# First chunk's attention in single precision, gate logits from transposed rows, weights' low halves by TensorE

## The chip, the cores and the metric

One core of a Trainium2 chip runs the whole program. The metric is the time of one execution on the device in microseconds. The core has five engines with a queue each: TensorE (PE, products; PEld is its loading of weights), VectorE (DVE), ScalarE (ACT), GpSimd (POOL) and SyncE (SP, which here issues most DMA transfers).

## The reference

Three stages follow each other; inputs and output are 32-bit floats but for `w_in` and `w_out`, which are stored as 64-bit floats.

```python
# 1: gated linear attention, q, k, v of 4 batches x 8 heads x 768 steps x 40
m_new = np.maximum(f_gate[:, :, t] + m, i_gate[:, :, t])
C = f_stab * C + i_stab * np.einsum('bhd,bhe->bhde', vt, kt)
n = f_stab * n + i_stab * kt
y[:, :, t] = sigmoid(o_gate) * (C @ qt) / np.maximum(np.abs(n @ qt), 1.0)
# 2: x = y as 3072 tokens x 320
h = x @ w_in                       # 320 x 2048
x = (h * sigmoid(h)) @ w_out       # 2048 x 320
# 3: one of 8 experts per token
logits = x @ w_gate
expert_idx = np.argmax(logits, axis=1)
out[mask] = gate_w[mask, None] * (np.maximum(xe @ w1[e], 0.0) @ w2[e])
```

The choice of the expert must be that of the reference, so products keep nearly 32-bit precision. The kernel does this with 16-bit floats in pairs: a value is a high half and a low half (the value less its high half), and a product is three products, high x high, high x low and low x high.

## The kernel before

**Attention.** The 768 steps are 6 chunks of 128. A unit (`unit(t)`, L616) is one chunk of one batch: t = 4 * chunk + batch, 24 units. It loads q, k, v and the output gate as 128 steps x 8 heads x 40. Units 0 to 3 are the first chunk. There `halves` (L648) scales q and k by ACT (L652), casts the high half by ACT (L653) and subtracts by POOL or DVE (L655) into tiles of 8 blocks of 128 columns; `turned` (L600) transposes these by 8 PE transposes (L612) and a copy (L614) in units 0 to 2, by a DMA transpose (L604) from unit 3 on. The scores of 4 heads are 4 products over 120 rows (L724), the decay weights of the first chunk come from products with masks (L680 to L684), DVE multiplies both (L726), ACT and POOL split the result (L730, L732), values are 24 products of 41 columns (L752 to L754) and the state 24 more (L790 to L792, weights of 40 columns). DVE divides and gates (L757 to L780), and the result is transposed for the dense layer.

**Widening of the dense weights.** `conv_in` and `conv_rest` (w_in, 8 + 2 units) and `conv_out` (w_out, 10 units) each load 64-bit values, make 32-bit values by three integer steps on DVE (`narrow`, L836, L839, L842) in a bank of PSUM, cast the high half by ACT (L866 or L75) and subtract it by DVE (L868, L920).

**Fold.** `fold_out` (L925) multiplies w_out with w_gate, so that the second dense product has 8 more columns, which are the logits. For each of 16 pieces of w_out it makes 6 PE transposes (L939, L940), one copy (L942) and 8 products of 8 columns (L949).

**Dense layer.** `l1(t, g)` is 32 products of 128 columns (L990), ACT and DVE apply the gate (L992, L994), ACT and POOL or DVE split (L997, L998); four g per tile t of 128 tokens. `l2(t, g)` is 12 products of 328 columns (L1019 to L1021) that add into one bank over the four g.

**Routing and experts.** After four tiles `route` (L1040) takes the logits, finds the expert by DVE, counts places by two small PE products (L1077, L1078), scales the rows and writes each to its expert's place in `rows_x` by an indirect DMA (L1129). A slot is 128 rows of one expert: a DMA transpose fetches it (L1199), 64 products (L1226) and 24 (L1239 to L1241) compute it, an indirect DMA writes it out (L1256). 28 slots run; five of them (`EARLY`) hold rows known before the last chunk is routed and stand first. The experts' weights are loaded and split while the kernel runs (`load_e`, L1142).

**What sets the order.** Every operation is a call of `op` with its engine, an assumed duration, what it reads and writes, and a rank. `Plan` (L115) lays all of them out in a list per engine by these assumptions, in up to eight passes that change the ranks, and writes the programs in that order. The table `RK` holds the first ranks. Each engine executes its list in order.

Of the kernel before, what the change touches and what calls it, by code (L numbers as in the profile page):

```python
# [20 lines left out]
SQ = 256.0  # L21
# [7 lines left out]
    tiles=19.85, win=71.01, dwin=4.64, wout=-64.58, dwout=5.8, u0=48.58, u1=136.74, u2=-181.17, u3=-847.73,  # L29
    lead1=223.69, lead=261.63, l1c=-202.11, l2c=-47.42, l2=113.07, gates=135.36, load=113.69, state=-161.3, route=-200.66,  # L30
# [83 lines left out]
class Plan:  # L114
# [8 lines left out]
    IDLE, WARM = 1500, 3000  # L123
# [164 lines left out]
def mlstm_moe_kernel(ctx, tc, q, k, v, ig, fg, og, w_in, w_out, w_gate, w1, w2, out):  # L288
# [17 lines left out]
    NO = DM + E  # L306
# [13 lines left out]
    groups = dict(l0=[0, 1], l1=[0, 1, 2], l2=[(3, 0), (4, 128)], s1=[0, 1, 2, 5, 6, 7], at=[5, 6, 7], gt=[2], wt=[2], pg=[(2, 480)])  # L320
# [3 lines left out]
    def bank(kind, *shape):  # L324
# [5 lines left out]
        hi = lo + (128 if kind == "pg" else 1536 if kind in ("wt", "l2") else 2048)  # L330
# [10 lines left out]
    A = [Region(const, f"A{i}", 20992 if i == 3 else 20480) for i in range(8)]  # L341
# [4 lines left out]
    ident16 = const.tile([128, 128], F16, name="ident16")  # L346
    E_t = const.tile([128, NC, BH], F32, name="E_t")
# [15 lines left out]
    X2 = Region(const, "X2", 4 * 1312)  # L363
# [11 lines left out]
    Ks_b = [a4.cut([128, H, 128], F16) for _ in range(2)]  # L375
# [17 lines left out]
    wo_b = [A[3].cut([128, 2, NO], F16) for _ in range(NF)]  # L393
    x2_b = [X2.cut([128, NO], F32) for _ in range(B)]
    row_b = [RO.cut([128, RW], F32) for _ in range(3)]
# [8 lines left out]
    xT_b = [W2.cut([128, 6, 128], F16) for _ in range(5)]  # L404
    hh_b = [[W2.cut([128, 2, 4, 128], F16) for _ in range(2)] for _ in range(2)]
# [16 lines left out]
    wT_b = [A[1].cut([128, 5, 128], F16) for _ in range(2)]  # L422
# [7 lines left out]
    mneg = a6.cut([128, 4, CH], BF16)  # L430

    pe, ve, ac, po, sp = nc.tensor, nc.vector, nc.scalar, nc.gpsimd, nc.sync

# [4 lines left out]
    op("POOL", 1200, c_pool, W=["ident"], rank=-20)  # L438

# [13 lines left out]
    def c_pool3():  # L453
        for x in Qs_b + Ks_b:
            po.memset(x.ap[:, :, 120:128], 0.0)
# [4 lines left out]
    op("POOL", 1500, c_pool3, W=[*Qs_b, *Ks_b, *v_b, *yy_b], rank=-18)  # L460

    def c_pool4():
# [10 lines left out]
        for x in row_b:  # L473
            po.memset(x.ap, 0.0)
        po.memset(row_b[0].ap[:, 385:386], 2.0 * NONE)
    op("POOL", 5000, c_pool4, W=["tok", "ebase", "tri", "cum", "rev", *row_b], rank=90, after=60)

    EARLY = [(0, 0), (0, 1), (1, 0), (1, 1), (1, 2)]

    def fill_rows():  # L480
        sp.dma_start(
            out=rows_x.rearrange("(e r) w -> r e w", e=E)[0:128],
            in_=row_b[0].ap.unsqueeze(1).to_broadcast([128, E, RW]),
        )
    op("SP", 1200, fill_rows, R=[row_b[0]], W=["rows"], rank=120, lag=2500, move=6400, after=120)
    for e, n in EARLY:
        def fill_early(e=e, n=n):
            o = e * ER + 128 * (n + 1)
            sp.dma_start(out=rows_x[o:o + 128, :], in_=row_b[0].ap)
        op("SP", 600, fill_early, R=[row_b[0]], W=["rows"], rank=121, lag=2500, move=800, after=121)  # L490

# [18 lines left out]
    def gates(c0, c1, rk):  # L510
# [49 lines left out]
        ps, kp = bank("gt", 128, 3, n * BH)  # L560
# [39 lines left out]
    def turned(t, a, z, n, rank):  # L600

        flat = a.ap.rearrange("p x c -> p (x c)")
        if t >= B - 1:
            op("SP", 1300, lambda: sp.dma_start_transpose(out=z.ap, in_=flat), R=[a], W=[z], rank=rank,  # L604
               lag=2800, move=225 * n)
# [10 lines left out]
    def unit(t):  # L616
# [6 lines left out]
        qT, kT = qT_b[i2], kT_b[i2]  # L623
        lam = lam_b[i2]
# [6 lines left out]
        for j, (x, d) in enumerate(((k, kr), (q, qr), (v, vr), (og, orr))):  # L631
            def load(x=x, d=d):
                sp.dma_start(out=d.ap[:, :, 0:D], in_=src(x, c, b))
            op("SP", 600, load, W=[d], rank=ld + (0, 0.1, 4, 6)[j], lag=2200, move=1050, after=ld - 10)
        if c > 0:
# [4 lines left out]
            ], R=["lam_d"], W=[*lam], rank=ld + 3, lag=2500, move=1860)  # L640
# [365 lines left out]
    def l2(t, g):  # L1006
        rk = pos(t) + 4 * g + RK["l2c" if t < B else "l2"]
        c, b = divmod(t, B)
        if g == 0:
            yb[t] = bank("l2", 128, NO)  # L1010
# [259 lines left out]
    for t in range(2, B):  # L1270
        unit(t)
# [242 lines left out]
```

## Time and profile before

| | us |
|---|---|
| three runs | 663.04, 663.45, 664.49; median 663.45 |
| profiled execution | 664.25, of which the span from first to last instruction is 662.6 |
| PE busy | 619.2 (93% of the span) |
| DVE busy | 500.8 (76%) |
| ACT busy | 408.4 (62%) |
| POOL busy | 320.8 (48%) |
| DMA moved | 103.27 MB, 156 GB/s on average |

A group's busy time is the time in which at least one of its instructions ran, so neighbours that overlap in a pipeline are not counted twice within a group. A product's own duration is longer than the distance to the next one; costs of runs are taken from distances of starts. The chain that ended last is PE for 81% of the span.

### The profile page before, as it was taken

The numbers are of one execution on the slowest core, as the hardware profiler recorded it, in microseconds if no ns is written. First come the engines' busy times: TensorE is split into PE (matmuls) and PEld (weight loads), VectorE is DVE, ScalarE is ACT, GpSimd is POOL, SyncE is SP. The second block draws the span as 40 slices with busy tenths as digits, with TensorE's granted clock in tenths as the row PEclk, the third lists the DMA queues.
The fourth block names the chain that finished last, engine by engine and source line by source line (L and its number), as shares of the span: only waits on it lengthen the run. The fifth ranks groups of instructions, "written<-read, shape, count | busy, mean of one in ns | idle before, by whom it ended". The sixth has DMA issues, their size and how long they took to land.

```text
span 662.6 us, 21228 instructions
## 1 busy us (share of the span) xinstructions
PE 619.2 (93%) x8493; PEld 526.8 (80%) x8494; DVE 500.8 (76%) x1014; ACT 408.4 (62%) x839; POOL 320.8 (48%) x455
## 2 busy tenths in 40 slices
PE   2488999999999999989999999999999999999992
PEld 2366888878888888878888889888888888888881
DVE  6997698748887899798888978857678675776650
ACT  4776688738797778677878655635335543644430
POOL 3735367727766786576765555421431322223231
PEclk9666799999999999999999999999999999999997
DMA  8999276898987788978955534375398999877710
GB/s 205 236 254 198 57 117 130 179 225 170 174 153 142 131 156 150 148 149 119 177 124 111 102 93 110 103 143 155 105 227 198 225 228 187 207 202 195 173 63 16
DMA packets 255909, 103.27 MB, mean 156 GB/s; under 512 B 193173, under 2 KB 251480, under 8 KB 255800
## 3 DMA queue, kind: packets, MB, share of 16 engines
q1 hardware_dynamic: 236728, 76.55, 60.0%
q10 hardware_dynamic: 16192, 16.59, 8.9%
q0 software_dynamic: 2880, 8.68, 4.1%
q8 instruction: 68, 1.11, 0.7%
q14 instruction: 41, 0.34, 0.2%
HBM read 68.76 MB, written 11.98 MB: 122 GB/s over the span
## 4 chain that ended last, share of the span: by engine, by line
PE 81%; DMA 8%; DVE 5%; ACT 2%; issue 1%; POOL 1%; SPq 1%; ACTq 0%; POOLq 0%; DVEq 0%
PE PS L990 24%; PE PS L1226 13%; PE PS L1019 7%; PE PS L1020 7%; PE PS L1021 7%; PE PS L1239 4%; PE PS L1241 4%; PE PS L1240 4%; DMA SG<-in_moe_w_dram 2%; PE PS L724 2%; DMA X<-in_moe_w_dram 1%; PE PS L939 1%; DMA A<-A 1%; PE PS L940 1%; DMA A<-in_k_dram 1%
## 5 line engine op out<-in xcount | busy, mean ns | idle before, releaser
L990 PE MATMUL PS<-A,A 128*128 128x128 f16 x3072 | 193.2, 221 | 0.6 <-DVE A L994 0.5
L990 PEld LDWEIGHTS <-A 128*128 128x128 f16 x3072 | 179.5, 99 | 4.7 <-issue 0.8
L1226 PE MATMUL PS<-W,A 128*128 128x128 f16 x1792 | 116.5, 219 | 0.4 <-issue 0.2
L1226 PEld LDWEIGHTS <-A 128*128 128x128 f16 x1792 | 108.3, 98 | 8.1 <-issue 0.4
L1019 PE MATMUL PS<-A,A 128*128 128x328 f16 x344 | 104.1, 303 | 0.0
L1021 PE MATMUL PS<-A,A 128*128 128x328 f16 x344 | 104.1, 302 | 0.0
L1020 PE MATMUL PS<-A,A 128*128 128x328 f16 x344 | 104.0, 302 | 0.0
L1256 POOL DMA_INDIRECT out_dram<-W,sid x28 | 29.4, 1052 | 124.2 <-DVE W L1244 52.0
L1228 ACT ACTIVATE W<-PS 128x512 f16<-128x512 f32 x56 | 32.9, 594 | 79.7 <-PE PS L1226 56.5
L992 ACT ACTIVATE A<-PS 128x512 f32<-128x512 f32 x96 | 56.8, 592 | 33.2 <-PE PS L990 24.6
L994 DVE SCALAR_TENSOR_TENSOR A<-A,PS 128x512 f32<-128x512 f32 x96 | 65.0, 679 | 8.3 <-ACT A L992 8.0
L997 ACT CAST A<-A 128x512 f16<-128x512 f32 x86 | 52.5, 613 | 25.1 <-DVE A L994 13.4
L1241 PE MATMUL PS<-A,W 128*128 128x320 f16 x224 | 67.0, 299 | 0.3 <-issue 0.3
L1239 PE MATMUL PS<-A,W 128*128 128x320 f16 x224 | 67.0, 299 | 0.1
L1240 PE MATMUL PS<-A,W 128*128 128x320 f16 x224 | 67.0, 299 | 0.0
L732 POOL TENSOR_TENSOR A<-A 128x512 f16<-128x512 f32 x33 | 39.2, 1190 | 43.4 <-ACT A L730 43.4
L1230 DVE SCALAR_TENSOR_TENSOR W<-PS,W 128x512 f16<-128x512 f32 x56 | 38.2, 688 | 27.9 <-ACT W L1228 27.8
L671 ACT ACTIVATE A<-A,bias_t 128x128 f32<-128x128 f32 x160 | 56.1, 394 | 1.0 <-POOL A L642 1.0
L998 POOL TENSOR_TENSOR A<-A,A 128x512 f16<-128x512 f32 x30 | 35.1, 1168 | 36.4 <-ACT A L997 36.0
L726 DVE SCALAR_TENSOR_TENSOR A<-PS,A 128x512 f32<-128x512 f32 x48 | 32.8, 684 | 21.3 <-PE PS L724 19.9
L998 POOL TENSOR_TENSOR A<-A 128x512 f16<-128x512 f32 x29 | 37.4, 1291 | 23.7 <-ACT A L997 23.7
L1021 PEld LDWEIGHTS <-A 128*128 128x128 f16 x344 | 33.6, 98 | 14.3
(251 smaller groups left out, 1362.5 us busy)
## 6 DMA issues: line engine op xcount, KB each, us to landing
A<-lam_d SPq DMA_DIRECT2D x40, 256.0 KB
SG<-in_moe_w_dram ACTq DMA_DIRECT2D x18, 320.0 KB
A<-in_moe_w_out_dram SPq DMA_DIRECT2D x10, 512.0 KB
SG<-in_moe_w_dram ACTq DMA_DIRECT2D x18, 256.0 KB
SG<-in_moe_w_dram SPq DMA_DIRECT2D x14, 320.0 KB
A<-in_moe_w_in_dram SPq DMA_DIRECT2D x8, 512.0 KB
A<-in_q_dram SPq DMA_DIRECT2D x24, 160.0 KB
A<-in_k_dram SPq DMA_DIRECT2D x24, 160.0 KB
```

What stands on the lines that cost most here:

```text
L671: ac.activation(out=lam[h // 4].ap[:, h % 4, :], in_=x, func=AF.Exp, bias=bias_t[:, c, b * H + h:b * H + h + 1])
L990: pe.matmul(ps[:, f, :], a, x, start=(n == 0), stop=(n == len(terms) - 1))
L992: op("ACT", act(512), lambda: ac.activation(out=th.ap, in_=ps, func=AF.Tanh, scale=0.5 * HS), R=[kk], W=[th], rank=rk)
L994: op("DVE", dve(512), lambda: ve.scalar_tensor_tensor(out=th.ap, in0=th.ap, scalar=1.0, in1=ps, op0=ALU.add, op1=ALU.mult), R=[kk], W=[th] ...
L998: op(DP, dp(512), lambda m: m.tensor_tensor(out=G.ap[:, 1], in0=th.ap, in1=G.ap[:, 0], op=ALU.subtract), R=[th], W=[G], rank=rk + 2, port= ...
L1019: pe.matmul(ps, gh, w[:, 0, :], start=(f == 0), stop=False)
L1020: pe.matmul(ps, gh, w[:, 1, :], start=False, stop=False)
L1021: pe.matmul(ps, gl, w[:, 0, :], start=False, stop=(f == NF - 1))
L1226: pe.matmul(ps[:, jj, :], l, m, start=(n == 0), stop=(n == len(terms) - 1))
L1239: pe.matmul(ps, hh[:, 0, f % 4, :], x[:, 0, :], start=(f == 0), stop=False)
L1240: pe.matmul(ps, hh[:, 0, f % 4, :], x[:, 1, :], start=False, stop=False)
L1241: pe.matmul(ps, hh[:, 1, f % 4, :], x[:, 0, :], start=False, stop=(f == NF2 - 1))
```

## The change

It does the following.

- The first chunk's attention (units 0 to 3) is computed with 32-bit products: q and k are transposed as they are, 4 transposes of 128 x 128 each (pairs of heads in 64 rows each), scores are 8 products over 40 rows (heads of a pair in different rows of the array), values and state 8 products each. The splitting in halves, its tiles and the two transposes by DMA of unit 3 go.
- `fold_out` and its tiles go; `l2` has 320 columns. `route` is now in two parts. The first scales a chunk's rows and splits them, as before, and SP transposes each of the four by DMA; the second forms the logits by 32 products of 8 columns on PE from the transposed rows and goes on as before. The last chunk has rows and tiles of its own.
- For the low halves of w_in and w_out PE subtracts the high half inside PSUM by a product with a negative scaled identity (`rest`), and ACT or DVE casts the result. The parts of `conv_rest` stay. w_in gets a second bank; three products at the start open the banks.
- Seven early slots in place of five (two of expert 2, whose weights are loaded by `load_all` ahead of them); the zero rows of `rows_x` are written by fewer and larger transfers.
- State products of later chunks load 128 weight columns in place of 40.
- The first ranks and some assumed durations have other values, so the lists of all engines are in another order throughout.

```diff
-    lead1=223.69, lead=261.63, l1c=-202.11, l2c=-47.42, l2=113.07, gates=135.36, load=113.69, state=-161.3, route=-200.66,
+    lead1=113.09, lead=1032.66, l1c=-437.46, l2c=-463.45, l2=-163.58, gates=-736.39, load=-73.54, state=-65.11, route=-284.86,
...
-    IDLE, WARM = 1500, 3000
+    IDLE, WARM = 600, 3400
...
-    EARLY = [(0, 0), (0, 1), (1, 0), (1, 1), (1, 2)]
+    EARLY = [(0, 0), (0, 1), (1, 0), (1, 1), (1, 2), (2, 0), (2, 1)]
...
+        def whole_turned(a, z, r):
+            flat = a.ap.rearrange("p h d -> p (h d)")
+            ps, kk = bank("at", 128, 512)
+            def go():
+                for i in range(4):
+                    x = slice(i * 128, (i + 1) * 128)
+                    pe.transpose(ps[:, x], flat[:, x], ident)
...
+        if c == 0:
+            whole_turned(kr, kT, p)
+            whole_turned(qr, qT, p + 0.5)
...
+            def pairs():
+                for j in range(4):
+                    x = slice(j * 128, j * 128 + 128)
+                    for g in range(2):
+                        r = slice(64 * g, 64 * g + D)
+                        pe.matmul(two[g][0][:, j, :], single(kT)[r, x], single(qT)[r, x], start=True, stop=True)
...
+                if c == 0:
+                    pe.matmul(pv[:, h, :], lam[h % 2].ap[:, h // 2, :], vr.ap[:, h, :], start=True, stop=True)
+                    continue
...
+                    if c == 0:
+                        pe.matmul(ps[0:D, h, :], kr.ap[:, h, 0:D], vw.ap[:, h, :], start=True, stop=True)
+                        continue
+                    kh, kl = K.ap[:, h * 128:h * 128 + 128], K.ap[:, h * 128 + D:h * 128 + D + 128]
...
-    cv_b = [PS.cut([128, 512], F32, at=2048 * i) for i in (3,)]
+    cv_b = [PS.cut([128, 512], F32, at=2048 * i) for i in (3, 2)]
...
+    def opened():
+        for x in cv_b + cvo_b:
+            pe.matmul(x.ap, ident16, ident16[:, 0:1].to_broadcast([128, 512]), start=True, stop=True)
...
+    def rest(mid, i, hi, lo, scale, keys, rk):
+        flat = mid.ap if len(hi.shape) == 2 else mid.ap.rearrange("p (a b) -> p a b", a=hi.shape[1])
+        op("PE", 220, lambda: pe.matmul(flat, less[i], hi, start=False, stop=True, skip_group_check=True),
+           R=["less", *keys], W=[mid], rank=rk)
+        op(AD, ad(512), lambda m: scaled(nc, m, lo, flat, scale), R=[mid], W=keys, rank=rk)
...
-        op("DVE", dve(512), lambda: ve.scalar_tensor_tensor(
-            out=w[:, 3:5, :], in0=x, scalar=SWI, in1=w[:, 0:2, :], op0=ALU.mult, op1=ALU.subtract
-        ), R=[mid, k[0]], W=[k[2]], rank=rk)
+        rest(mid, 0, w[:, 0:2, :], w[:, 3:5, :], SWI, [k[0], k[2]], rk)
...
-    def fold_out(q):
...
-            def trans(j=j, ps=ps):
...
-            def fold(j=j, wT=wT):
...
+            op("SP", 1300, lambda b=b, r16=r16: sp.dma_start_transpose(out=xr[b].ap, in_=r16[:, 0:768]),
+               R=[row], W=[xr[b]], rank=rb, lag=2800, move=1270)
+        yield
+        pl, kl = bank("at", 128, nb, E)
+        def logits():
+            h, l = wg16[:, 0], wg16[:, 1]
+            for b in range(nb):
+                z = xr[b].ap
+                terms = [(0, h[:, 0]), (1, h[:, 1]), (2, h[:, 2]), (0, l[:, 0]), (1, l[:, 1]),
+                         (3, h[:, 0]), (4, h[:, 1]), (5, h[:, 2])]
+                for n, (j, w) in enumerate(terms):
+                    pe.matmul(pl[:, b, :], z[:, j, :], w, start=(n == 0), stop=(n == len(terms) - 1))
+        op("PE", 8 * 27 * nb, logits, R=[*xr[0:nb], "wg"], W=[kl], rank=rk + 1.8 * dr)
```

The order on DVE early in the start, when the first units of weights are widened (A_66 are values of w_in, A_67 of w_out, A_71 scores, W_94 gates). Before:

```order
L920 SCALAR_TENSOR_TENSOR A_69<-PS,A_69 128x8x64
L726 SCALAR_TENSOR_TENSOR A_71<-PS,A_71 128x512
L836 TENSOR_SCALAR PS<-A_67 128x512
L842 SCALAR_TENSOR_TENSOR PS<-A_66,PS 128x512
L839 SCALAR_TENSOR_TENSOR PS<-A_67,PS 128x512
L519 SCALAR_TENSOR_TENSOR W_94<-W_94 32x640
L842 SCALAR_TENSOR_TENSOR PS<-A_67,PS 128x512
```

Now (L889, L892, L895 are the three integer steps, L768 the scores):

```order
L892 SCALAR_TENSOR_TENSOR PS<-A_66,PS 128x512
L768 SCALAR_TENSOR_TENSOR A_71<-PS,A_71 128x512 x2
L889 TENSOR_SCALAR PS<-A_67 128x512
L895 SCALAR_TENSOR_TENSOR PS<-A_66,PS 128x512
L892 SCALAR_TENSOR_TENSOR PS<-A_67,PS 128x512
L889 TENSOR_SCALAR PS<-A_66 128x512
L895 SCALAR_TENSOR_TENSOR PS<-A_67,PS 128x512
```

The subtractions of L920 are gone from between the integer steps, and w_in and w_out alternate.

The order on PE at the first unit: before, the start of the list goes on with the fold (A_69 is w_out, A_67 its transposed piece):

```order
L939 MATMUL PS<-ident_75,A_69 128x128
L940 LDWEIGHTS A_69
L940 MATMUL PS<-ident_75,A_69 64x128
L949 LDWEIGHTS A_67
L949 MATMUL PS<-wg_81,A_67 128x8
```

Now the first unit's scores (L758), values (L797) and state (L840) stand with the subtractions for w_out and w_in (L908):

```order
L908 LDWEIGHTS less_77
L908 MATMUL PS<-A_69,less_77 128x512
L758 MATMUL PS<-A_71 128x128 x8
L908 LDWEIGHTS less_76
L908 MATMUL PS<-A_68,less_76 128x512
L797 MATMUL PS<-A_70,A_71 128x41 x8
L840 MATMUL PS<-A_70,A_67 40x41 x8
```

No transposes of weights are left on PE, and each widened unit has one instruction there instead.

The order on SP at the last chunk: before, the fetches of the early slots end and the loads of weights and the tables follow:

```order
L1199 DMA_TRANSPOSE W_94<-rows_x 128x6x128
L1200 DMA xm_126<-rows_x 128x2
L1153 DMA SG<-in_moe_w_dram 128x2x256
L1154 DMA SG<-in_moe_w_dram 64x256
L1155 DMA SG<-in_moe_w_dram 64x256
```

Now the last early fetches are followed by the four transposes of the last chunk's rows (L1110):

```order
L1253 DMA xm_131<-rows_x 128x2
L1252 DMA_TRANSPOSE A_72<-rows_x 128x6x128
L1253 DMA xm_132<-rows_x 128x2
L1110 DMA_TRANSPOSE A_71<-A_72 128x6x128 x4
L1201 DMA X_93<-in_moe_w_dram 128x2x256
```

What moved is that loads behind L1110 wait until the rows are scaled.

## Rows read from the trace of the kernel before

**Rows 1.** The page, 40 slices: busy share in tenths, granted clock, DMA share.

```profile
PE   2488999999999999989999999999999999999992
...
PEclk9666799999999999999999999999999999999997
DMA  8999276898987788978955534375398999877710
```

**Rows 2.** Stretches: length, then busy us per engine, granted clock, DMA share, GB/s.

```profile
0.00:38.06 38.06, 17.01 (x154) 13.28 (x155) 30.51 (x66) 25.55 (x49) 20.80 (x40) 0.79 0.98 238
38.06:99.26 61.20, 55.82 (x729) 44.82 (x729) 49.74 (x93) 45.54 (x91) 27.58 (x47) 0.77 0.74 140
99.26:650.20 550.94, 546.33 (x7614) 468.72 (x7612) 419.96 (x856) 337.29 (x701) 270.06 (x364) 1.00 0.74 155
650.20:662.60 12.40, 0.00 (x0) 0.00 (x0) 0.55 (x1) 0.00 (x0) 2.38 (x4) 0.63 0.06 20
```

**Rows 3.** Groups on PE: busy us, mean ns | idle before, releasers.

```profile
L939 PE MATMUL PS<-ident,A 128*128 128x128 f16 x64 | 11.0, 266 | 4.2 <-ACT A L942 4.0
L940 PE MATMUL PS<-ident,A 128*64 128x128 f16 x32 | 9.1, 284 | 0.0
L612 PE MATMUL PS<-ident,A 128*128 128x128 f16 x66 | 8.5, 301 | 7.6 <-ACT A L777 3.9 <-POOL A L655 2.4 <-ACT A L614 0.9
...
L949 PE MATMUL PS<-wg,A 128*128 128x8 f16 (+1 forms) x128 | 7.0, 170 | 0.8 <-ACT A L942 0.8
```

**Rows 4.** Timeline of PE: start us, busy us; state, values, first dense product.

```profile
22.20 0.22 PE L790 MATMUL PS<-A,A 128*40 128x41 f16 x1 [1.54 <-ACT A L652]
...
23.16 0.22 PE L752 MATMUL PS<-A,A 128*128 128x41 f16 x1
...
38.06 1.55 PE L990 MATMUL PS<-A,A 128*128 128x128 f16 x16
```

**Rows 5.** Timeline of PE: 32-bit products, and 512 columns of 16 bits.

```profile
12.49 0.63 PE L570 MATMUL PS<-A 32*128 32x32 f32 x2
13.05 0.39 PE L612 MATMUL PS<-ident,A 128*128 128x128 f16 x2
...
34.65 1.80 PE L566 MATMUL PS<-ident,W 32*128 32x32 f32 x15
36.38 0.61 PE L680 MATMUL PS<-A,A 128*128 128x512 bf16 x1
36.78 0.31 PE L683 MATMUL PS<-A 128*128 128x128 bf16 x1
```

**Rows 6.** Groups on DVE, and its timeline at the eighth product group.

```profile
L920 DVE SCALAR_TENSOR_TENSOR A<-PS,A 128x512 f16<-128x512 f32 x10 | 6.8, 684 | 2.2 <-ACT A L75 2.2
L868 DVE SCALAR_TENSOR_TENSOR A<-PS,A 128x512 f16<-128x512 f32 x8 | 5.4, 681 | 3.2 <-ACT A L866 3.2
...
L942 DVE COPY A<-PS 128x640 f16<-128x640 f16 x3 | 1.5, 492 | 3.1 <-PE PS L940 2.0 <-PE PS L949 1.1
...
99.26 0.68 DVE L994 SCALAR_TENSOR_TENSOR A<-A,PS 128x512 f32<-128x512 f32 x1
```

**Rows 7.** Groups on PE with 328 and with 320 columns.

```profile
L1019 PE MATMUL PS<-A,A 128*128 128x328 f16 x344 | 104.1, 303 | 0.0
...
L1239 PE MATMUL PS<-A,W 128*128 128x320 f16 x224 | 67.0, 299 | 0.1
```

**Rows 8.** Timeline of PE: products of 8 columns, a run of 24.

```profile
81.45 0.42 PE L949 MATMUL PS<-wg,A 128*128 128x8 f16 x8
...
261.98 0.20 PE L790 MATMUL PS<-A,A 128*40 128x41 f16 x1
...
262.58 0.18 PE L792 MATMUL PS<-A,A 128*40 128x41 f16 x1
```

**Rows 9.** SP: transposes by DMA; landing times of transfers with rows_x.

```profile
L604 SPq DMA_TRANSPOSE A<-A x63: 1212/1247/4469, 56.3 to 418.5; - x63
...
DMA to landing us min/median/max: 2.9/4.2/6.8
```

More of the change, by code (lines that the diff above doesn't have):

```diff
@@ L339, in pos @@
         return T0 + TT * t
-    A = [Region(const, f"A{i}", 20992 if i == 3 else 20480) for i in range(8)]
+    A = [Region(const, f"A{i}", 20640 if i == 4 else 20480) for i in range(8)]
     home = [0, 1, 4, 5, 6, 2, 3, 7]
@@ L346, in mlstm_moe_kernel @@
     ident16 = const.tile([128, 128], F16, name="ident16")
+    less = [const.tile([128, 128], F16, name=f"less{i}") for i in range(2)]
     E_t = const.tile([128, NC, BH], F32, name="E_t")
@@ L438, in mlstm_moe_kernel, with c_less @@
     op("POOL", 1200, c_pool, W=["ident"], rank=-20)
+    def c_less():
+        for x, y in zip(less, (SWI, SWO)):
+            ac.activation(out=x, in_=ident16, func=AF.Copy, scale=-1.0 / y)
+    op("ACT", 600, c_less, R=["ident"], W=["less"], rank=-10)
     def c_pool2():
@@ new lines, in whole_turned @@
+        def whole_turned(a, z, r):
[5 more added lines that the diff above has]
+                    pe.transpose(ps[:, x], flat[:, x], ident)
+            op("PE", 4 * 110, go, R=[a, "ident"], W=[kk], rank=r)
+            op(AD, ad(512), lambda m: (m.copy if m is ac else m.tensor_copy)(out=single(z), in_=ps),
+               R=[kk], W=[z], rank=r)
@@ L1009, in l2 @@
         if g == 0:
[L1010 removed]
+            yb[t] = bank("l2", 128, DM)
         ps, kk = yb[t]
@@ new lines, in route, with count, place @@
+        op("DVE", 760, hot, R=["rev"], W=[(kr, "ld"), ("oh", c, b0)], rank=rk + 2.2 * dr)
+        def count():
+            for t in range(t0, t1):
+                ve.tensor_tensor(out=cum[:, t + 1, :], in0=cum[:, t, :], in1=oh[:, t, :], op=ALU.add)
+        op("DVE", 170 * nb, count, R=[("oh", c, b0)], W=["cum"], rank=rk + 2.4 * dr)
+        pr, kk = bank("at", 128, nb, E)
+        def place():
+            pe.matmul(pr, ones, cum[:, T, :], start=True, stop=False)
+            pe.matmul(pr, tri, oh[:, T, :], start=False, stop=True)
@@ L1135, in send @@
                 puts.append(p_)
-            op("POOL", 1050, send, R=[row, (kr, "di"), "rows", "early"], W=[("put", t)], rank=rb, lag=2500, move=600)
+            op("POOL", 1050, send, R=[row, (kr, "di"), *filled, "early"], W=[("put", t)], rank=rb, lag=2500, move=600)
     stcount = [0]
@@ L1313, in mlstm_moe_kernel @@
                 load_e(e, g, we_b[e], x, 12)
+        if t == B or t == NTT - 1:
+            for x in row_b[2:] if t == B else row2_b:
+                op("POOL", 80, lambda x=x: po.memset(x.ap.bitcast(F16)[:, 704:768], 0.0), W=[x], rank=pos(t) - 8)
         if t % B == 0 and t > 0:
-            route(t // B - 1, 0, B, pos(t) + RK["route"], 1.0)
-            if t == NTT - B:
+            ways = route(t // B - 1, 0, B, pos(t) + RK["route"], 1.0)
+            next(ways)
+        if t % B == 1 and t > 1:
+            next(ways, None)
+            if t == NTT - B + 1:
                 pc, kc = bank("at", 128, E)
@@ L1338, in mlstm_moe_kernel @@
         l2(NTT - 1, g)
-    route(NC - 1, 0, B, pos(NTT) + 12, 0.5)
+    for _ in route(NC - 1, 0, B, pos(NTT) + 12, 0.5):
+        pass
     end0 = pos(NTT) + 10
     for n, (e, i) in enumerate(early):
+        if e > 1 and e != early[n - 1][0]:
+            load_all(e, end0 + 2 + TS * n)
         slot(i, we_b[e], end0 + 2 + TS * n)
```

332 lines of the change are left out of this document (163 added, 169 removed).

## The prediction

> **What bounds the kernel now.** I read the 40 slices first, then the four stretches, then PE's groups, then the two instruction lists of PE and DVE in the first 100 us. The slices [rows 1] show PE at 9 tenths from the fifth slice to the last but one, with a granted clock of 0.6 to 0.7 in slices 2 to 5, a mixture of the two levels 1.2 and 2.4 GHz, and 2.4 GHz after that. The stretches [rows 2] put numbers on it. PE is busy 546.33 of the 550.94 us between 99.26 and 650.20, so what shortens this part must take work off PE or start it earlier. The last 12.40 us hold no PE work and the change does not touch them. PE's idle time lies in front: 21.05 us up to 38.06, where the first product of the dense layer starts [rows 4], and 5.4 us from there to 99.26. In this second stretch PE is busy 55.82 us at a granted clock of 0.77, and DVE is busy 49.74 of 61.20 us: DVE widens weights there, and PE fills the time with work that is there only because of the gate's fold [rows 3].
>
> I take as a milestone the eighth product group of the dense layer to reach DVE. It starts at 99.26 [rows 6]. After it PE has no gap to speak of, so the end moves by what this milestone moves, plus what the later PE work gains or loses.
>
> **The change, part by part.**
>
> *Fold removed.* The 96 transposes and 128 small products of the fold are busy 11.0, 9.1 and 7.0 us, 27.1 in all, and PE waited 5.0 us in front of them, mostly for the copies of their results [rows 3]. All of it lies before 99.26. With it go 16 copies, 13 on ACT and 3 on DVE of 0.49 us [rows 6].
>
> *First chunk, half precision removed.* Of the 66 transposes of L612 48 are of q and k, 48/66 of 8.5 is 6.2 us [rows 3]. State and value products come as runs of 24: one run is 23.16 - 22.20 = 0.96 us [rows 4], eight runs 7.7. Scores: 32 products at some 0.1, 3.2. Together 17.1 us. ACT and POOL lose the splitting in halves, which only shortens the chain to the first product.
>
> *First chunk, single precision added.* 32 transposes, 32 score products, 64 value and state products, 128 instructions. The trace has few such rows [rows 5]: 15 transposes of 32 x 32 from 34.65 to 36.38, 0.115 us each; one 32 x 32 product, recorded as two instructions, from 12.49 to 13.05, 0.56 us with its hand-over at both ends, 0.28 per record. For a transpose of 128 columns I take 0.23 (between 0.115 and four times that), 7.4 us. For a score product I take 0.28, since two of 40 rows each stand in different rows of the array, 9.0 us (0.14 to 0.56). For a value or state product of 41 columns I take 0.28 as well, since they stand in runs of eight and the hand-over is paid once, 17.9 us (0.115 to 0.56). The sum is 34.3 us; by the low ends 15.6, by the high ends 68.4.
>
> The row for one 32 x 32 product shows two records and two weight loads. The Trainium skill says (TensorE: Matmul & The Clock Gate, "LDWEIGHTS (loading the stationary operand)" and "Weight-path perf modes — Fast Weight Load (FWL) and DoubleRow") that a load of 128 columns takes about 107 ns and that the fast load is not used for 32-bit weights. That sets a floor under this part at either clock: an estimate from the page is 2 x 107 = 214 ns for a product even when nothing else holds it, 13.7 us for the 64. By the row it is 17.9, by the page the forecast would be some 4 us lower and could fall no further.
>
> *Low halves by PE.* The subtraction of the weights' high halves leaves DVE: 18 instructions, 10 of L920 and 8 of L868, 0.684 us each, 17 of them before 99.26, which is 11.6 us; DVE had waited 2.2 + 3.2 us in front of them for ACT [rows 6]. In their place stand 18 PE products of 512 columns, 36.78 - 36.38 = 0.40 us each at the low clock [rows 5], 7.2 us, and 18 evictions that ACT or DVE takes; in DVE's new order 3 of them stand ahead of the eighth product group, 2.0 us. ACT takes the others, about 0.6 us each, out of what it got back. The three products that open the banks run before anything else is ready and cost nothing; if they were late, 1.2 us.
>
> *What that does to the milestone.* DVE ahead of the eighth group: 11.6 + 1.5 - 2.0 = 11.1 us less work, and 5.4 us less waiting if ACT is no longer late, 16.5 in all. PE: 27.1 + 17.1 - 34.3 - 7.2 = 2.7 us less work and 5.0 less waiting, 7.7. The milestone follows the slower of the two in any one place, and PE partly has idle time to hide in. I take 12 us, the middle of 7.7 and 16.5. This is the one large term and is an estimate.
>
> *The dense layer's second product.* 320 columns in place of 328: by the rows of both shapes [rows 7] 104.1/344 goes to 67.0/224, 302.6 to 299.1 ns, and 3.5 ns x 1152 = 4.0 us less, all of it in the stretch that PE fills.
>
> *Logits from transposed rows.* 192 products of 8 columns on PE. Eight of the fold's at 81.45 are busy 0.42 us [rows 8]; 24 such runs are 10.1 us. In a run of 32 the ends are paid once: a run of 24 at full clock takes 0.026 per product (first to last start 262.58 - 261.98 = 0.60 us) [rows 8], so the ends are 0.42 - 8 x 0.026 = 0.21 and a run of 32 is 1.04, six runs 6.2 us. I take 6.2; between 5.0 (no ends) and 10.1.
>
> *24 more transposes by DMA.* SP issues four per chunk at 1.247 us, 5.0 us in which the loads behind them wait [rows 9]; the loads of a unit are issued well ahead, so this costs nothing where they stay so, and up to 5 us once where they don't. POOL's work is the same but for its order. The wait that is added is PE's, for the four transposed tiles. A row that SP writes or reads lands 2.9 to 6.8 us after its issue [rows 9]. From the last product of a chunk to its logits go two steps of ACT, three of DVE, one of POOL, four issues and a landing: some 3.5 + 5 + 4 to 7 us, 13 to 16. Between the two PE has its other products in the new order, 16 us of them in the last chunk and 18 to 30 in the others by the durations of before. So it is hidden, with nothing to spare at the end; I take 1.5 us. In the last chunk seven slots in place of five stand ready before the others need it.
>
> The rest (pads, zero rows, the split of the gate's weights, tables of fetches, 128 weight columns in place of 40 for state, whose records are spaced alike) I cost at nothing: each is hidden beside PE at 546.33 of 550.94. The new loads' order puts the first layer's weights ahead of the second's; it is within the 12 us.
>
> The sum, against the profiled execution's own 664.25 us: 664.25 - 12 - 4.0 + 6.2 + 1.5 = 655.95. The median of the three runs is 0.8 lower, and so is the forecast: **655 us**.
>
> **The rivals.**
>
> *The clock comes early.* PE ran its 55.82 us of the second stretch at 0.77 [rows 2]. With the fold and its waits gone PE has fewer gaps and its products come densely. If it reaches full clock in that stretch, 55.82 x 0.23 = 12.8 us are to be had, some 8 of them beyond my 12: 647. For it speaks that the granted clock is 0.77 for the stretch and 1.00 for all that follows, where PE has no gaps [rows 2]; against it that the single-precision work of four units is spread over the same time.
>
> *Single precision is dear.* If score, value and state products cost 0.56 us, 96 of them are 26.9 us more, PE becomes the bound of the start, and some 10 of the 26 us of idle time absorb a part: 7.7 - 16.9 makes the milestone 9 us later, 664.25 + 9 + 3.7 - 0.8 = 676. From about 0.42 us each the kernel is slower than before. For it speaks the only row there is; against it that this row is a lone product.
>
> *The logits wait.* If PE stands for 2 us or more in each chunk, because SP's queue or a busy DMA brings the tiles late, 6 x 2 are lost on top: 667. For it speaks the DMA share of 7 to 9 tenths up to half of the span [rows 1], against it the PE work that the order puts between.
>
> *The loads set the start.* The DMA share is 0.98 up to 38.06 [rows 2] and the bytes stay the same. If weights come no earlier, the milestone moves 3 us and the rest eats it: 664. Against it: the share falls to 0.74 in the second stretch, where most of the widening is done.
>
> **How the numbers follow.** My case gets 0.55, the early clock 0.20, dear single precision 0.10, waiting logits 0.08, loads 0.07. My case's own range is 649 to 661. The range of 8 in 10 reaches from 644 (early clock with the low prices) to 667 (waiting logits, loads). A difference under 0.2%, 1.3 us, is about what a measurement here cannot tell from none. Faster: my case, the early clock and half of the loads' case, 0.78; within 0.2% 0.05; slower 0.17.
>
> **What would show it.** The eighth eviction of the dense layer's products should start at about 87 us, PE should be free of the fold, and no wait of PE for the transposed rows should pass 2 us. The single-precision products should stand in runs of eight that take about 2.2 us. The milestone at 96 or later, or runs of eight over 3.4 us, would make the forecast wrong; so would a gap of PE over 5 us anywhere after 100 us.

## The result, and the profile after

The changed kernel takes 668.94 us (median of 20 runs, 664.00 to 675.59), the kernel before 664.31 (20 runs, 662.16 to 667.06). The ratio is 1.0062, with a 95% interval of 1.0044 to 1.0080: it is slower by 0.6%, where 655 us were forecast. One of the 20 runs (675.59) and one of the four of e5_xm (677.55) were in a slower state and count in no ratio. The profiled execution took 669.95 us; its span is 668.3 us, 5.7 more than the span before.

The slices of the changed kernel's page, as [rows 1]:

```profile
PE   3888999999899999999999999959799999999993
...
PEclk9996999999999999999999999969899999999997
DMA  8996687999999898997799544372734899878820
```

The start is better than before: PE is at 8 tenths from the second slice. Two holes have come, in the 27th and the 29th slice, where [rows 1] have nines, and the clock falls there.

The clock's digits of the first slices do not tell PE's speed. The first record of the granted clock in this trace is at 41.51 us (18.61 in the trace of before), and where there is none the views count full clock. The products themselves show the low level up to 41.5: one unit's 32-bit scores (16 records) take 2.35 us ahead of it and 1.16 us behind it.

```profile
19.02 2.35 PE L758 MATMUL PS<-A 40*128 40x128 f32 x16
...
41.70 1.16 PE L758 MATMUL PS<-A 40*128 40x128 f32 x16
```

The stretches of the changed kernel (length, then busy us on PE, PEld, DVE, ACT, POOL, granted clock, DMA share, GB/s): up to the first dense product, up to the eighth product group at DVE, up to 425 us, the stretch with the holes, the experts, the tail.

```profile
0.00:32.90 32.90, 19.93 (x101) 13.42 (x102) 27.21 (x57) 13.44 (x27) 9.56 (x33) 1.00 0.96 227
32.90:88.58 55.68, 51.19 (x558) 43.80 (x558) 45.09 (x87) 38.80 (x80) 17.76 (x38) 0.88 0.76 168
88.58:425.00 336.42, 329.32 (x5026) 287.91 (x5024) 280.49 (x595) 246.97 (x553) 214.94 (x274) 1.00 0.85 161
425.00:480.00 55.00, 42.22 (x489) 34.93 (x488) 22.78 (x40) 17.31 (x31) 10.85 (x16) 0.89 0.57 117
480.00:657.10 177.10, 176.86 (x2267) 152.52 (x2264) 115.52 (x225) 73.32 (x116) 44.88 (x79) 0.99 0.69 170
657.10:668.30 11.20, 0.00 (x0) 0.00 (x0) 0.35 (x1) 0.00 (x0) 1.89 (x4) 0.60 0.06 20
```

The first product of the dense layer starts at 32.90 (38.06 before [rows 4]), the eighth group at 88.58 (99.26 before [rows 6]): the milestone moved by 10.7 us, 12 were forecast. Behind it nothing of this is left. Between 425 and 480 PE is busy 42.22 of 55 us, where [rows 2] had 546.33 of 550.94 for everything behind the milestone.

The time can be split without a remainder. PE's own time, counted by the distance from one start to the next without the waits, is 619.7 us before and 620.0 now; it contains what PE loses at the low clock level. PE's waits of over 0.15 us are 26.1 and 17.5 us up to the milestone, 3.8 and 6.7 from there to some 425 us, 0.6 and 12.7 behind that, and the tail behind PE's last product is 12.4 and 11.4. So the span grew by 0.3 - 8.6 + 2.9 + 12.1 - 1.0 = 5.7 us. The question is the 12.1.

The longest waits of PE (total, times, longest), and below them the three holes on its timeline (start, busy; in brackets the wait before it):

```profile
PE PS L1018 <- DVE A L1022: 6.1, 3, 5.1
PE PS L1292 <- DVE W L1297: 4.9, 1, 4.9
PE PS L1047 <- ACT A L1025: 2.7, 1, 2.7
```

```profile
435.64 1.06 PE L1018 MATMUL PS<-A,A 128*128 128x128 f16 x16
441.77 1.87 PE L1018 MATMUL PS<-A,A 128*128 128x128 f16 x16 [5.08 <-DVE A L1022]
446.39 0.45 PE L1047 MATMUL PS<-A,A 128*128 128x320 f16 x1 [2.75 <-ACT A L1025]
...
478.52 0.42 PE L1292 MATMUL PS<-A,W 128*128 128x320 f16 x1 [4.87 <-DVE W L1297]
```

The run of 16 products behind the first hole takes 1.87 us in place of 1.06: PE is at the lower clock level there until some 451 us. Counted by distances, the products behind the holes cost some 4.4 us more than the same products elsewhere, so the holes cost 12.7 + 4.4 = 17.1 us.

DVE and ACT are named as releasers, but neither was busy. ACT's timeline at the first two holes shows who kept them (ACTq are transfers that ACT issues):

```profile
429.06 0.60 ACT L1020 ACTIVATE A<-PS 128x512 f32<-128x512 f32 x1 [0.48 <-PE PS L1018]
433.09 0.38 ACTq L1201 DMA_DIRECT2D SG<-in_moe_w_dram  x1
438.53 0.48 ACTq L1202 DMA_DIRECT2D SG<-in_moe_w_dram  x1
439.11 0.55 ACTq L1203 DMA_DIRECT2D SG<-in_moe_w_dram  x1
439.76 0.54 ACTq L1204 DMA_DIRECT2D SG<-in_moe_w_dram  x1
440.40 0.60 ACT L1020 ACTIVATE A<-PS 128x512 f32<-128x512 f32 x1 [10.74 <-issue]
440.90 0.61 ACT L1025 CAST A<-A 128x512 f16<-128x512 f32 x1
441.75 0.37 ACTq L1201 DMA_DIRECT2D SG<-in_moe_w_dram  x1
443.92 0.47 ACTq L1202 DMA_DIRECT2D SG<-in_moe_w_dram  x1
...
445.72 0.62 ACT L1025 CAST A<-A 128x512 f16<-128x512 f32 x1 [4.21 <-DMA SG<-in_moe_w_dram]
```

ACT issues two groups of four loads of expert weights (`load_e`). The four instructions themselves take 2 us, but ACT stands in front of the first and the second for 3.4 and 5.1 us, and the eviction L1020 behind them, for which PE waits, comes at 440.40. What the loads wait for is in the program's list of waits. The kernel's framework has eight semaphores for all transfers of SP and ACT and uses them in turn; a transfer waits until the one eight places ahead of it, which used the same semaphore, has landed. At this place ACT's list reads (a wait named DMAHW is one of the eight):

```
L1020 ACTIVATE A_73<-PS 128x512 [waits PE_49,Activation_49]
L1201 DMA SG<-in_moe_w_dram 128x2x256 [waits DMAHW4_49,DVE_49]
L1202 DMA SG<-in_moe_w_dram 64x256 [waits DMAHW7_49]
L1203 DMA SG<-in_moe_w_dram 64x256 [waits DMAHW0_49,DVE_49]
L1204 DMA SG<-in_moe_w_dram 128x2x320 [waits DMAHW2_49,DVE_49]
L1020 ACTIVATE A_72<-PS 128x512 [waits PE_49,Pool_49]
```

The transfers eight places ahead are those of SP's early fetches of rows (L1252 a transpose, L1253 a small copy), which start only when the rows have been put, at 429.85. The chain that ended last runs through them:

```profile
426.08 3.75 DMA rows_x<-W,di
429.85 1.23 SPq L1252
431.12 0.56 SPq L1253
431.74 1.21 SPq L1252
...
433.62 1.21 SPq L1252
...
439.97 3.92 DMA A<-rows_x
443.92 0.47 ACTq L1202
...
467.59 7.22 DMA A<-A
474.83 0.47 ACTq L1202
```

The load at 433.09 waits for the copy issued at 431.12, the one at 438.53 for the third transpose (433.62), the one at 443.92 for the sixth (439.97 + 3.92 = 443.89). The trace records the semaphores, too, and bears this out: the copy lands at 433.01 and the third transpose at 438.51, each on the semaphore that the load behind it uses next. The third hole is the same again with the four transposes that the new routing gave to SP (L1110): the last is issued at 467.59 and lands at 474.81, ACT's second load follows at 474.83, and ACT's eviction behind them, for which DVE and PE wait, at 476.69.

In the kernel before, ACT's loads stand beside SP's fetches as well:

```profile
440.92 0.61 ACT L997 CAST A<-A 128x512 f16<-128x512 f32 x1
442.15 0.42 ACTq L1153 DMA_DIRECT2D SG<-in_moe_w_dram  x1
...
445.51 0.37 ACTq L1156 DMA_DIRECT2D SG<-in_moe_w_dram  x1
445.92 0.62 ACT L997 CAST A<-A 128x512 f16<-128x512 f32 x1 [4.39 <-DMA SG<-in_moe_w_dram]
```

There ACT stood for 4.39 us and PE had no wait: its list held enough other products.

### The profile page after: what moved, and what is told of

Its sections match the earlier page's. It is cut to its first block, busy times and chain, and to the rows that moved or that the text cites. A ratio compares the mean times of both kernels' runs of the same rounds, so it can differ in the third digit from the quotient of the medians.

```text
span 668.3 us, 21038 instructions
## 1 busy us (share of the span) xinstructions
PE 619.5 (93%) x8435; PEld 532.6 (80%) x8435; DVE 491.4 (74%) x1001; ACT 389.8 (58%) x804; POOL 299.9 (45%) x441
## 4 chain that ended last, share of the span: by engine, by line
PE 70%; DVE 10%; DMA 9%; SPq 3%; issue 3%; ACT 3%; POOL 2%; ACTq 1%; POOLq 0%; DVEq 0%
PE PS L1018 18%; PE PS L1279 14%; PE PS L1049 6%; PE PS L1047 6%; PE PS L1048 6%; PE PS L1292 4%; PE PS L1294 4%; PE PS L1293 4%; DMA A<-A 4%; DMA A<-in_k_dram 2%; DVE A L768 1%; PE PS L766 1%; SPq L1252 1%; DVE A L1022 1%; PE PS L758 1%
## 5 line engine op out<-in xcount | busy, mean ns | idle before, releaser
L1018 PE MATMUL PS<-A,A 128*128 128x128 f16 x3072 | 196.4, 222 | 6.5 <-DVE A L1022 6.1
L1279 PE MATMUL PS<-W,A 128*128 128x128 f16 x1664 | 107.1, 220 | 0.0
L1047 PE MATMUL PS<-A,A 128*128 128x320 f16 x344 | 103.5, 301 | 2.7 <-ACT A L1025 2.7
L1049 PE MATMUL PS<-A,A 128*128 128x320 f16 x344 | 103.5, 301 | 0.1
L1048 PE MATMUL PS<-A,A 128*128 128x320 f16 x344 | 103.5, 301 | 0.0
L1020 ACT ACTIVATE A<-PS 128x512 f32<-128x512 f32 x96 | 56.5, 592 | 44.2 <-PE PS L1018 21.5
L1022 DVE SCALAR_TENSOR_TENSOR A<-A,PS 128x512 f32<-128x512 f32 x96 | 64.6, 678 | 20.7 <-ACT A L1020 20.1
L1026 POOL TENSOR_TENSOR A<-A 128x512 f16<-128x512 f32 x32 | 38.9, 1216 | 48.0 <-ACT A L1025 47.7
L768 DVE SCALAR_TENSOR_TENSOR A<-PS,A 128x512 f32<-128x512 f32 x48 | 32.5, 684 | 18.7 <-PE PS L766 13.5
L1026 POOL TENSOR_TENSOR A<-A,A 128x512 f16<-128x512 f32 x26 | 33.4, 1286 | 24.2 <-ACT A L1025 24.1
L777 POOL TENSOR_TENSOR A<-A 128x512 f16<-128x512 f32 x27 | 33.1, 1228 | 24.7 <-ACT A L775 24.5
```

The lines of the kernel that those rows point to most:

```text
L1018: pe.matmul(ps[:, f, :], a, x, start=(n == 0), stop=(n == len(terms) - 1))
L1020: op("ACT", act(512), lambda: ac.activation(out=th.ap, in_=ps, func=AF.Tanh, scale=0.5 * HS), R=[kk], W=[th], rank=rk)
L1022: op("DVE", dve(512), lambda: ve.scalar_tensor_tensor(out=th.ap, in0=th.ap, scalar=1.0, in1=ps, op0=ALU.add, op1=ALU.mult), R=[kk], W=[th] ...
L1026: op(DP, dp(512), lambda m: m.tensor_tensor(out=G.ap[:, 1], in0=th.ap, in1=G.ap[:, 0], op=ALU.subtract), R=[th], W=[G], rank=rk + 2, port= ...
L1047: pe.matmul(ps, gh, w[:, 0, :], start=(f == 0), stop=False)
L1048: pe.matmul(ps, gh, w[:, 1, :], start=False, stop=False)
```

## The experiments

Theory A is what was just read: the turns of the semaphores hold ACT, and the evictions behind it hold PE. Theory B: the transfers are slow there whoever issues them. Theory C: the refitted order as such costs the time. Theory D: ACT can issue nothing while SP's transposes are under way. Each number below is a median, with the ratio to the kernel before on the same chip.

### e1_sp: three groups of loads issued by SP

```diff
-        self.out = sorted(best[1], key=lambda x: x[0])
+        moved = {2378, 2383, 2480}
+        self.out = [(t, end, i, "SP" if i in moved else e) for t, end, i, e in sorted(best[1], key=lambda x: x[0])]
```

> Three of the groups of four loads of expert weights that ACT issues beside SP's fetches of rows and transposes (at 433.1, 441.8 and 474.3 us of the changed kernel) are issued by SP at the same place of the order; nothing else moves. Theory A (ACT stands in its queue until the transfer of SP eight places earlier has landed, because SP and ACT use the same eight semaphores in turn, and the evictions behind it hold PE): PE's 12.7 us of idle time between 436 and 479 us go, and with them some 4.4 us in which PE ran at the low clock after each gap: 668.9 - 17 = 652 us, between 649 and 656; ACT stands less than 2 us at a time between 425 and 480. Theory B (the transfers themselves are slow there, since transposes and loads share the DMA engines, and it does not matter who issues them): the weights land as late as before, PE waits for them or for the rows: 665 to 672.

Measured: 649.28 us (5 runs, 648.59 to 651.75), ratio 0.9794 (0.9771 to 0.9817). Theory A's number, and faster than both kernels. The same stretches of its profile, from its own eighth group on:

```profile
87.27:425.00 337.73, 331.41 (x5066) 290.23 (x5064) 283.80 (x599) 250.11 (x558) 216.60 (x276) 1.00 0.87 162
425.00:480.00 55.00, 55.00 (x758) 48.36 (x756) 32.46 (x73) 21.54 (x39) 16.02 (x26) 1.00 0.64 145
480.00:636.40 156.40, 156.16 (x1960) 133.47 (x1958) 103.75 (x190) 66.95 (x105) 38.08 (x66) 1.00 0.76 179
```

PE is busy 55.00 of 55 us where it was 42.22, at the full clock. Only twelve loads differ, in their issuer and, by it, in their time and turn: SP issues the first four from 423.95 us on, ahead of its first fetch, and the next four from 431.16 on, between its second fetch and its third. Theory B is out: those four land 2.9 to 4.1 us after their issue, the first four of ACT in the changed kernel 2.4 to 3.3, so the transfers are not faster here, but no eviction stands behind them.

PE's list is the same product by product, so the two profiled executions can be laid side by side. The one of e1 is 2.9 us ahead at 420 us, where the lists have not differed yet, and 20.9 ahead at 485: the holes cost 18.0 us, 17.1 of which were read above.

### e2_late: ACT keeps the loads, behind the dense layer's last evictions

```diff
+        for ops, mark in (((2378, 2383), 2258), (tuple(range(2379, 2383)) + tuple(range(2384, 2388)), 2299)):
+            mine = [x for x in out if x[2] in ops]
+            out = [x for x in out if x[2] not in ops]
+            n = 1 + next(n for n, x in enumerate(out) if x[2] == mark)
+            out[n:n] = mine
```

> ACT keeps its loads, but the two groups at 433.1 and 441.8 us stand behind the last evictions of the dense layer in ACT's order, and the casts of these weights behind the first evictions of the experts; the third group (474.3 us) stays. Theory A: the first two gaps of PE (5.1 and 2.75 us, and some 2.8 us of low clock behind them) go, the third (4.9 us and 1.6) stays or moves: 668.9 - 10.6 = 658, between 655 and 663. Theory B: the loads are later still, PE waits for weights: 668 or more.

Measured: 656.99 us (6 runs, 653.97 to 658.44), ratio 0.9895 (0.9871 to 0.9918). Two holes are gone, one of 4.8 us is left (PE waits for the evictions of a slot at 456 us). As theory A had it: the loads are later and the kernel is faster, because what PE waits for stands ahead of them.

### e3_early5: five early slots

```diff
-    EARLY = [(0, 0), (0, 1), (1, 0), (1, 1), (1, 2), (2, 0), (2, 1)]
+    EARLY = [(0, 0), (0, 1), (1, 0), (1, 1), (1, 2)]
```

> One part undone: five early slots as in the kernel before, in place of seven; all lists are laid out anew for it. Theory A: SP has ten transfers in place of fourteen at that place and expert 2's weights are not wanted there, so ACT's loads wait less: PE idle between 425 and 480 us under 6 us in place of 12.7, 658 to 665. Theory B: the same gaps, 667 to 671. Theory C (the new first ranks are worse for the whole program): nothing gained, 667 to 672.

Measured: 668.23 us (6 runs, 667.41 to 673.08), ratio 1.0078 (1.0051 to 1.0105). A miss for theory A's time: PE's waits between 425 and 480 fell to 5.5 us as expected (busy 49.55 of 55), but waits of 3.4 and 1.3 us came at 169 and 187 us and 2.7 and 1.2 us at 482 and 500, in the newly laid out lists. The hold itself is still there, only elsewhere on ACT:

```profile
423.62 0.37 ACTq L1201 DMA_DIRECT2D SG<-in_moe_w_dram  x1
424.02 0.54 ACTq L1202 DMA_DIRECT2D SG<-in_moe_w_dram  x1
432.99 0.47 ACTq L1203 DMA_DIRECT2D SG<-in_moe_w_dram  x1
```

By the list of waits the third load is in turn behind the small copy that belongs to SP's first fetch. SP issues that copy at 430.85, since it waits for the rows itself; ACT stands from 424.6 on, six us before that transfer has even been issued. So the number of fetches is not the lever, and a turn passes on whatever the transfer ahead in it waits for.

### e4_ranks: the first ranks of the kernel before

```diff
-    tiles=19.85, win=310.54, dwin=120.43, wout=56.12, dwout=-21.22, u0=-372.07, u1=-36.9, u2=-978.22, u3=-878.97,
+    tiles=19.85, win=71.01, dwin=4.64, wout=-64.58, dwout=5.8, u0=48.58, u1=136.74, u2=-181.17, u3=-847.73,
...
-    IDLE, WARM = 600, 3400
+    IDLE, WARM = 1500, 3000
```

> One part undone: the table of first ranks and the two assumed durations of the kernel before, with all else of the change. Theory C (the refit of the order costs the time): 655 or less. Theory A: the ranks are not the cause as such; the new lists put other work beside SP's fetches, so the time follows the gap that PE has there, between 658 and 675, and PE's idle time between the first put of chunk 4 and the first early slot accounts for the difference to e1.

Measured: 675.83 us (6 runs, 672.96 to 682.27), ratio 1.0194 (1.0156 to 1.0233). Theory C is out. Theory A's range was left by 0.8 us, and its account was too narrow: the eighth group starts only at 110.11, PE waiting 15.9 us for the casts of ACT ahead of the new subtractions, so most of the loss is at the start. ACT is held here too, from 447.1 to 457.0. The refit of the order is worth some 20 us at the start to the new code.

### e5_xm: the small copies on POOL

```diff
     def fetch_slot(row0, rk, keys, i=None):
+        m = sp if i is None else po
...
-            sp.dma_start(out=xm, in_=r[:, 384:386])
+            m.dma_start(out=xm, in_=r[:, 384:386])
```

> The changed kernel, ACT's loads where they were; only the seven small transfers (128 x 2) that follow SP's early row fetches are issued by POOL, which has semaphores of its own. So ACT's loads of the first two groups take their turn behind other transfers: the second to fourth load of the first group behind the first, second and third row fetch, those of the second group behind the fourth to seventh. Theory A (turns of eight semaphores): the first group ends some 3 us earlier, the second not later than the landing of the seventh fetch; PE's first gap 1 to 3 us in place of 5.1, the second near 0, the third as before: 660 to 664; each load of ACT starts when the named fetch has landed. Theory D (no issue of ACT goes through while SP's transposes are under way): all eight loads of ACT start after the last of the seven fetches has landed, and the gaps stay: 667 to 670.

Measured: 673.93 us (4 runs, 667.09 to 677.55), ratio 1.0131 (1.0095 to 1.0168). The time is a miss: the first hole went, but the second grew to 6.1 us, and the third is 4.3 in the profiled execution, which took 667.09 us; why the other runs are slower by up to 10 us no profile shows. The starts of ACT's loads decide between A and D all the same:

```profile
432.10 0.48 ACTq L1202 DMA_DIRECT2D SG<-in_moe_w_dram  x1
...
433.82 0.41 ACTq L1204 DMA_DIRECT2D SG<-in_moe_w_dram  x1
...
437.38 0.39 ACTq L1201 DMA_DIRECT2D SG<-in_moe_w_dram  x1
...
441.81 0.38 ACTq L1204 DMA_DIRECT2D SG<-in_moe_w_dram  x1
```

The landing of the seventh fetch, in the chain that ended last:

```profile
437.12 4.58 DMA A<-rows_x
```

SP issues the seven transposes from 428.08 to 437.12, the last landing 4.58 us later at 441.70 (437.12 + 4.58). The first group of ACT's loads goes out in the middle of them, and the very last load follows the seventh landing by 0.1 us, its place in the turns. By the trace's semaphores each of the seven loads that the expectation pairs with a fetch starts 0.02 to 0.1 us after that fetch has landed, the three of the first group after 432.08, 432.93 and 433.74. Theory D is out. The turns also explain the second hole: ACT's second group now waits for the last four fetches.

### e6_before: control, the kernel before with its group issued by SP

```diff
+        moved = {2451}
+        self.out = [(t, end, i, "SP" if i in moved else e) for t, end, i, e in sorted(best[1], key=lambda x: x[0])]
```

> Control: in the kernel before, the one group of loads that ACT issues beside SP's fetches (442.2 us) is issued by SP, as in the first experiment. Theory A: ACT's wait of 4.4 us there goes, but PE had work in front of it and no gap, so nothing is gained: 663 to 666, within 0.2% of before. If it gains over 1%, the wait cost the kernel before as well and the change did not expose it.

Measured: 665.76 us (12 runs), 666.24 for the kernel before beside it, ratio 0.9984 (0.9971 to 0.9997). As expected within 0.2%: the hold costs only where PE has nothing in front of it. With the hold taken out of both, the change is worth 0.9794 / 0.9984 = 0.981, some 12.6 us.

### e7_dve: the low halves by DVE again

```diff
-        op("PE", 220, lambda: pe.matmul(flat, less[i], hi, start=False, stop=True, skip_group_check=True),
+        op("PE", 220, lambda: None,
...
-        op(AD, ad(512), lambda m: scaled(nc, m, lo, flat, scale), R=[mid], W=keys, rank=rk)
+        op(AD, ad(512), lambda m: ve.scalar_tensor_tensor(
+            out=lo, in0=mid.ap if len(hi.shape) == 2 else flat, scalar=scale, in1=hi, op0=ALU.mult, op1=ALU.subtract
+        ), R=[mid], W=keys, rank=rk)
```

(On top of e1's edit; all of these instructions are put on DVE.)

> The first experiment's kernel, but the low halves of w_in and w_out are again subtracted by DVE straight out of PSUM (one instruction in place of PE's product and an eviction), in the same place of the lists. By the prediction DVE sets the start: ahead of the eighth product group DVE gets some 14 instructions of 0.68 us more, 9 us, and PE loses 6.4 us of work: the eighth group 5 to 10 us later than in the first experiment, 653 to 659. Rival (PE sets the start): the eighth group at the same time or up to 6 us earlier, 644 to 650.

Measured: 654.46 us (5 runs), ratio 0.9823 (0.9797 to 0.9849), against 0.9794 for e1. The eighth group starts at 87.98, against 87.27 in e1. Ahead of it DVE is busy 7.9 us more, and PE has 13 products less. The 0.7 us at the milestone speak against DVE alone as the bound (5 to 10 were expected), but the time lies in the range of DVE's case and not in the rival's, and the milestone differs by some 4 us between executions of one list (last section). So neither engine is shown to set the start alone. In time the part is worth 0.3%, with intervals that overlap.

### e8_double: the first chunk's value and state products issued twice

```diff
-                    pe.matmul(pv[:, h, :], lam[h % 2].ap[:, h // 2, :], vr.ap[:, h, :], start=True, stop=True)
+                    for _ in range(2):
+                        pe.matmul(pv[:, h, :], lam[h % 2].ap[:, h // 2, :], vr.ap[:, h, :], start=True, stop=True)
...
-                        pe.matmul(ps[0:D, h, :], kr.ap[:, h, 0:D], vw.ap[:, h, :], start=True, stop=True)
+                        for _ in range(2):
+                            pe.matmul(ps[0:D, h, :], kr.ap[:, h, 0:D], vw.ap[:, h, :], start=True, stop=True)
```

(On top of e1's edit.)

> The first experiment's kernel, with each of the first chunk's single-precision value and state products issued twice: 128 more records, 12.6 us of PE by the changed kernel's rows. If PE bounds the start, the eighth group is 10 to 13 us later and the time 659 to 662; if these products stand in PE's idle time of the start (17 us up to the eighth group), 3 to 7 us later, 652 to 657.

Measured: 662.02 us (12 runs, 660.52 to 665.93), ratio 0.9952 (0.9932 to 0.9971), which is 0.0158 or 10.5 us over e1. The eighth group starts at 94.51, 7.2 us later. The added products take 11.5 us by distances. In time most of them count, so PE's work in the start is not hidden; the 7.2 at the milestone are in doubt by the same 4 us and lie just above the second expectation.

## Why the prediction was wrong, point by point

**The step that failed** is the one that moves work to SP: "The loads of a unit are issued well ahead, so this costs nothing where they stay so, and up to 5 us once where they don't", with 1.5 us for all stalls. It named the queue of SP and the loads behind L1110 in it. It did not ask who else takes turns with SP's transfers. ACT does, and behind ACT's loads stand the evictions that PE waits for. The runs show 12.7 us of waits and 4.4 us at the lower clock in its place; taking twelve loads off ACT gives back 17.8 us by the ratios to the kernel before (1.0062 and 0.9794; 19.7 between the medians), for the 17.1 read from one trace. The rest of the change was worth more than forecast: 12.6 us by e1 and e6, where 8.3 were added up. The forecast's condition, "a gap of PE over 5 us anywhere after 100 us" would make it wrong, is what came (5.08).

None of the rivals had this. The one that waits for the logits gave 667, near the measured time, by another mechanism: PE's longest wait for the transposed tiles is 0.73 us (L1122 in the rows of groups below), well under the 2 us that it needed. Its transposes did cost time, but through ACT's turn (the third hole).

**The milestone** was right in size, 10.7 for 12, and half wrong in its reason. "The milestone follows the slower of the two" took 16.5 us on DVE's side into the middle. In e7 7.9 us more of DVE's work, with PE relieved, moved it by 0.7; in e8 11.5 us more of PE's moved it by 7.2 and the time by 10.5. So PE's work counts, and DVE's is not shown to. PE's own time up to the milestone fell by 2.1 us (forecast 2.7), its waits by 8.6. That the 2.1 is near the 2.7 is in part luck: with the same list up to there e1 and e2_late have 66.6 and 67.8 us of own time, this execution 71.1 (73.2 before), since PE ran at the low level for different stretches.

**The terms on PE**, by distances of starts over the whole span, forecast and measured (at whatever clock level they ran): fold -27.1 and -22.0; half precision of the first chunk -17.1 and -16.1; single precision +34.3 and +24.9; subtractions +7.2 and +6.6, with 1.5 for the opening products that were forecast at nothing; 320 columns -4.0 and -4.3; logits +6.2 and +5.0. The busy time of groups, from which the fold's 27.1 came, counts the end of each run and is too high by a fifth for short runs. The rows of single precision in the changed kernel:

```profile
L797 PE MATMUL PS<-A,A 128*128 128x41 f32 x64 | 9.5, 314 | 0.0
...
L758 PE MATMUL PS<-A 40*128 40x128 f32 x64 | 5.8, 323 | 0.0
L1122 PE MATMUL PS<-wg,W 128*128 128x8 f16 x160 | 4.9, 166 | 0.7 <-DMA W<-W 0.7
L840 PE MATMUL PS<-A,A 128*40 128x41 f32 x64 | 3.7, 221 | 0.0
```

Each product stands as two records. By distances of starts the 32 value products (L797, 128 weight columns) take 9.06 us, 0.283 each. That this is the forecast's 0.28 is luck, since it is a mean over both clock levels: the first unit's eight, at the low level, take 3.73 us, 0.467 each, those of the other units 1.70 to 1.86 us, 0.21 to 0.23 each. A score product (L758) takes 5.63 / 32 = 0.176 in the mean, a state product (L840), with 40 weight columns, 3.54 / 32 = 0.111.

The run of 3.73 us is over the 3.4 us that the prediction named as a sign against it, but single precision did not make the kernel slower: all of it cost 24.9 us where 34.3 were forecast. The rival of dear single precision is out: the 96 products take 0.19 us in the mean, and only the eight at the low level pass its 0.42. The forecast took its rates of single precision from [rows 5], where the 15 transposes stand at a granted clock of 0.50, and did not reckon with the level.

The Trainium skill's floor (TensorE: Matmul & The Clock Gate, "LDWEIGHTS (loading the stationary operand)") goes by the weights' columns; the prediction applied its 214 ns for 128 columns to all 64 products and took it as a floor at either clock. The value product's 0.21 to 0.23 at the full level stands at it, the 0.467 at the low level is about twice that. The state product's 0.111 lies below, and the skill's own rule gives 2 x 40 / 1.2 = 67 ns for its 40 columns, an estimate that the row agrees with as a floor.

**The early clock** came in part, and not in every execution alike. The 0.88 of the stretch up to the milestone counts the time ahead of 41.51 us as full clock; with the low level that the products show there it is 0.80, an estimate from the records, where [rows 2] had 0.77. In e1 the same stretch has 0.87, and there the milestone stands at 87.27.

**Why the turns must wait**: the Trainium skill says (DMA: Bandwidth & Descriptors, "Why a DMA increments its semaphore by 16 and not by 1") that two transfers in flight on one semaphore can let a wait pass before the first has landed, and asks for one semaphore per slot in flight. The waits of the list are the price of sharing eight; no run here shows the failure that they prevent. The same page ("Issuing engines are not separate DMA queues") says that the issuing engine saves only the time to issue. The traces agree in e1, where the loads moved to SP and PE found its weights in time, without a wait between 425 and 480. But they show a price beside the time to issue: the first group of loads took ACT 2 us to issue, and ACT stood 8.5 us more for their turns.

## What to carry to other kernels

When a change adds transfers to one queue, look at what the other issuing engines share with it, and write down for each transfer on an engine that also computes which earlier transfer it takes turns with and what that one waits for; a load on ACT is free only where no eviction that PE needs stands behind it. A wait that is covered today, like the 4.39 us of ACT in the kernel before, is a debt that a refitted order can call in. Where two engines look as if they bound a stretch, double the work of one and take work from the other before putting a number between them, and set the answer against the scatter that executions of one list show there.

## What was not expected of the hardware

The start differs from execution to execution although these kernels have the same lists up to 420 us. The changed kernel and e2_late, the stretch from 50 us:

```profile
50.00:60.00 10.00, 8.20 (x54) 6.15 (x54) 9.54 (x19) 8.71 (x18) 2.43 (x5) 0.50 1.01 193
```

```profile
50.00:60.00 10.00, 9.05 (x88) 7.74 (x87) 8.25 (x18) 7.84 (x18) 4.01 (x7) 0.66 0.76 163
```

The granted clock from 50 to 60 us is 0.50 in one and 0.66 in the other (0.51 in e1_sp), and the eighth group starts at 88.58, 84.47 and 87.27. PE's own time for the same 659 records up to there is 71.1, 67.8 and 66.6 us, its waits are 17.5, 16.7 and 20.7. So between the first two the clock level makes most of the difference, 3.4 of 4.1 us; in e1 less time at the low level is nearly eaten by longer waits. Why the level falls in one execution earlier than in another stays open. A start with gaps carries a scatter of some 4 us, and the runs spread over 664.0 to 670.8 us for the changed kernel, but for the one at 675.6, and over 662.2 to 667.1 for the kernel before.
